# An mLSTM with a soft mixture of experts on one core: four regroupings of the instruction order

## The chip, the cores and the metric

One core of a Trainium2 chip runs the whole kernel in one launch. The metric is the device time of that core in microseconds (us), from one execution; the median of several executions is given for a kernel. Lower is better. TensorE, VectorE, ScalarE and GpSimd compute, SyncE (SP) issues the DMAs. Each engine takes its instructions in the order in which they were recorded, and waits where one needs another engine's result.

## What is computed

For 4 batches, 8 heads, 768 tokens and heads of 40 values, an mLSTM recurrence with stabilised exponential gates, its output gated and normalised; then the 320 values of a token (all heads) go through a soft mixture of 8 experts with 4 slots each.

```python
# attention part, per token t (per batch and head)
m_new  = maximum(f[t] + m, i[t])
f_stab = exp(f[t] + m - m_new);  i_stab = exp(i[t] - m_new);  m = m_new
C = f_stab * C + i_stab * outer(v[t], k[t])
n = f_stab * n + i_stab * k[t]
y[t] = sigmoid(o[t]) * (C @ q[t]) / maximum(abs(n @ q[t]), 1.0)

# soft mixture, x: 3072 tokens x 320
logits = x @ phi                                # 32 slots
d = softmax of logits over the tokens;  slot_input = d.T @ x
slot_out[e] = maximum(slot_input[e] @ w1[e], 0) @ w2[e]
c = softmax of logits over the slots;   out = c @ slot_out
```

All data is float32 (the output too). w1 and w2 are 10.5 MB each.

## The kernel before

**Steps.** The tokens of a batch are cut into 6 chunks of 128. A step is one chunk of one batch; the 24 steps go chunk by chunk with the four batches inside, so step i is chunk i // 4 of batch i % 4. Within a chunk the recurrence is done by matrices: a mask of decays times the products of queries and keys (the part inside the chunk), and the state of the earlier chunks times the queries (the part between chunks).

**What a step does, by function.** `expo(i)` (L304): TensorE multiplies two small matrices, RRt and LLt, into pe (L309), which holds the exponents of the decay mask; ScalarE makes the exponential, EWt (L311). `mix_rl(i)` (L317): ScalarE copies EWt's last column, rl, with which the keys are scaled. `scores(i)` (L347): TensorE, queries times keys into the bank psc, which has one buffer. `mix(i)` (L372): VectorE multiplies psc into EWt in place. `pv(i)` (L419): TensorE, EWt times values into the bank ph, which has one buffer. `inter(i)` (L360): TensorE, state times queries into pi; `inter_ops(i)` (L366): VectorE scales it with the decays eg into itt. `post1_ops(i)` (L427 to L431): VectorE adds itt to ph and forms the denominator's reciprocal den in three short instructions; `post2(i)` (L445): VectorE multiplies ph by the output gate sig. `gate(i)` (L456): sig times den gives the token output x; on GpSimd up to step 20 exclusive, on VectorE from there. `keys(i)` (L377): GpSimd scales the keys with rl into KRt. `state(i)` (L391, L393): TensorE, KRt times values into the bank pst; `state_dec(i)` (L399): GpSimd multiplies the state St by the decay dS; `state_ops(i)` (L406 on ScalarE for the first chunk, L407 on VectorE later): pst is added to St. `xtr(i)` (L466, L469): TensorE transposes x, ScalarE copies it to xT.

**Gates.** `gate_part` turns raw gates into the matrices' entries by scans and elementwise operations, for chunk 0, for chunks 1 and 2, and for chunks 3 to 5. The scans (L223, L228, L252) and L229 to L234 are VectorE's, L224 to L227 GpSimd's. For chunks 1 and 2, `nxt`, the first four go out before the loop and the rest, with `last_sums`, at the end of step 1. `chunk_ops(i)` puts a step's gates in place: `side` writes LLt (ScalarE, L270), `spread` writes RRt (VectorE, L277). The last chunks' operations are spread over steps 2 to 8 by the list PLATE.

**Decays.** `decays(c)`, at the end of steps 2, 4, 8, 9 and 10: TensorE transposes the gates of chunk c (L331), ScalarE makes eg of them (L332); except for the last chunk, TensorE multiplies the gates' last sums, rg (L335), and ScalarE makes dS (L336). Both products lie in one tile, pg, of the rotation pm: two PSUM buffers that pi, pt (from `xtr`), pl (the logits), pd, psl and pc share. The bank pst is 512 columns wide, of which the state's product uses 328.

**Mixture.** Groups of four steps: `logits_mm` (L474) into pl; running maximum nm (L491, L495); ScalarE's exponential dT and copy lt (L506, L514); dT transposed (L518), copied to d (L520); psl = d times x (L527), added to acc (L533). For the weights of the combination c: lt transposed, maximum subtracted (L544 to L549), exponential e (L553), the sum's reciprocal rsum (`comb_s_ops`, L574 to L576), e times rsum (`comb_n`, L583), split into a rounded part (`comb_hi`, ScalarE, L587) and a rest (`comb_lo`, GpSimd, L591), transposed into pc (L565), copied to cT (L569). In the loop a group's part of this stands in steps with i % 4 of 1, 2, 3 and 0; the multiplication by rsum stands in steps 7, 11, 15 and 19.

**The end.** Steps 22 and 23 (NL = 22, NL + 1) are written out behind the loop, with the last groups' mixture between them; then slot inputs (L882 to L907), the experts' two layers (`up`, `down`) and the combination with the output's DMAs (`combine`). The w2 weights come in 16 waves of 640 KB (`load_wave`), into buffers that the loop has done with; 11 of them are issued here. bk is the bank of psc under another name, pq and phe are that of pe.

**What sets the order.** The order is written by hand: `tc.manual_schedule()` keeps the order of recording on each engine, and the framework adds the waits for data and buffers. Waits between engines on PSUM are kept per bank: an engine that touches a bank waits until another engine's earlier access to the bank is done.

## Time and profile before

| | |
|---|---|
| median of 3 runs | 190.71 us (188.79 to 194.32) |
| the profiled execution | 188.0 us |
| its span, first to last instruction | 186.2 us |
| mean granted TensorE clock | 0.964 of full speed |
| moved by DMA | 47.42 MB, 255 GB/s over the span |

The profile is of one execution of the kernel, so the rows add up to 186.2 us, and the 1.8 us to 188.0 lie around them. Times in rows are us from the first instruction. PE is TensorE's matmul, PEld its weight load, DVE VectorE, ACT ScalarE, POOL GpSimd; a name such as EWt is a tile of the program, L372 a line of the kernel. A row's bracket tells how long the engine stood idle just before, and whose end released it. Idle time of an engine that nobody waits for costs nothing.

### The profile page before, as it was taken

Reading aid. Unit: us, or ns where it says so; the run is one execution under the profiler, and the core shown is the slowest. Engines: PE = TensorE matmul, PEld = TensorE weight load, DVE = VectorE, ACT = ScalarE, POOL = GpSimd, SP = SyncE. Lnnn points to the kernel's source line nnn. Section 1 sums busy time; section 2 is a strip of 40 time slices with the busy share of each in tenths; the row PEclk is TensorE's granted clock in tenths of the full one; section 3 lists DMA queues with packets and bytes.
Section 4 is the critical chain, followed back from the end, with each engine's and each line's share of the span. In section 5 each row is a group of like instructions: output and inputs, shape, how many; then the busy total and the mean of one; then the engine's idle time right before and its main releaser. Section 6 shows DMA issues by size and latency. Waiting matters only on the chain.

```text
span 186.2 us, 6239 instructions
## 1 busy us (share of the span) xinstructions
PE 159.5 (86%) x2594; PEld 117.3 (63%) x2594; DVE 124.1 (67%) x305; ACT 85.8 (46%) x205; POOL 63.1 (34%) x90
## 2 busy tenths in 40 slices
PE   7986657996896989997999989999978798999950
PEld 2554546885586867766877778777764442478740
DVE  6863786279879957479775997779688366323450
ACT  4888643656374544544445336634303432004340
POOL 8038058646336544046434443434211201100000
PEclk9999978999999699999999999999997899999996
DMA  5999998679968899766899989783869998001996
GB/s 173 306 315 367 314 328 279 193 218 376 268 199 271 217 338 302 227 220 175 303 344 293 278 253 364 210 274 100 256 214 364 362 364 267 0 4 57 293 305 194
DMA packets 27323, 47.42 MB, mean 255 GB/s; under 512 B 3184, under 2 KB 18288, under 8 KB 27296
## 3 DMA queue, kind: packets, MB, share of 16 engines
q1 hardware_dynamic: 27296, 47.03, 80.1%
q8 instruction: 20, 0.33, 0.8%
q14 instruction: 7, 0.06, 0.1%
HBM read 42.80 MB, written 4.23 MB: 253 GB/s over the span
## 4 chain that ended last, share of the span: by engine, by line
PE 69%; DVE 13%; ACT 8%; issue 4%; POOL 2%; DVEq 0%; ACTq 0%; POOLq 0%
PE psc L347 11%; PE ph L419 10%; PE pe L309 7%; PE pi L360 6%; PE pt L466 5%; PE pso L945 5%; PE pw L173 4%; DVE EWt L372 3%; PE pst L391 3%; PE po L975 3%; PE bk L917 2%; PE phh L917 2%; DVE RRt L277 2%; PE psl L527 2%; ACT xT L469 2%
## 5 line engine op out<-in xcount | busy, mean ns | idle before, releaser
L456 POOL TENSOR_TENSOR Xt<-sig,den 128x320 f32<-128x320 f32 x20 | 17.1, 856 | 53.1 <-DVE sig L445 53.1
L372 DVE TENSOR_TENSOR EWt<-psc,EWt 128x1024 f32<-128x1024 f32 x24 | 29.2, 1216 | 5.3 <-ACT rl L317 4.6
L347 PE MATMUL psc<-KQt 64*128 64x128 f32 (+1 forms) x384 | 28.6, 290 | 4.0 <-DVE EWt L372 1.9
L469 ACT COPY xT<-pt 128x384 f32<-128x384 f32 x23 | 10.9, 479 | 38.8 <-PE pt L466 38.8
L419 PEld LDWEIGHTS ph<-KVt,EWt 128*64 128x64 f32 x704 | 23.4, 143 | 8.2 <-issue 5.8
L347 PEld LDWEIGHTS psc<-KQt 64*128 64x128 f32 (+1 forms) x384 | 24.1, 192 | 6.4 <-DVE EWt L372 2.8
L311 ACT ACTIVATE EWt<-pe 128x512 f32<-128x512 f32 x48 | 26.0, 593 | 4.6 <-PE pe L309 4.4
L419 PE MATMUL ph<-KVt,EWt 128*64 128x41 f32 x704 | 26.0, 236 | 1.2 <-issue 1.2
L360 PE MATMUL pi<-St,KQt 104*64 104x82 f32 x320 | 15.7, 241 | 0.0
L377 POOL TENSOR_TENSOR KRt<-KVt,rl 128x320 f32<-128x320 f32 x20 | 14.7, 736 | 2.2 <-DMA KVt<-in_kv_dram 1.3
L366 DVE TENSOR_TENSOR itt<-pi,eg 128x328 f32<-128x328 f32 x20 | 10.0, 499 | 6.9 <-PE pi L360 5.7
L360 PEld LDWEIGHTS pi<-St,KQt 104*64 104x64 f32 x320 | 12.5, 136 | 2.3
L391 PE MATMUL pst<-KVt,KRt 128*64 128x41 f32 x160 | 12.8, 230 | 0.8 <-POOL KRt L377 0.7
L466 PE MATMUL pt<-cst,Xt 128*128 128x128 f32 x63 | 11.5, 296 | 2.0 <-DVE itt L366 2.0
L399 POOL TENSOR_TENSOR St<-St,dS 104x328 f32<-104x328 f32 x16 | 12.7, 794 | 0.1
L391 PEld LDWEIGHTS pst<-KVt,KRt 128*64 128x64 f32 x160 | 11.5, 142 | 1.3 <-POOL KRt L377 0.8
L309 PE MATMUL pe<-RRt,LLt 128*64 128x512 f32 (+1 forms) x24 | 9.0, 459 | 3.7 <-DVE RRt L277 2.3
L427 DVE TENSOR_TENSOR ph<-ph,itt 128x328 f32<-128x328 f32 x18 | 9.1, 504 | 3.6 <-PE ph L419 3.6
L591 POOL TENSOR_TENSOR E<-e,E 128x256 fp32r<-128x256 f32 x7 | 5.1, 735 | 14.4 <-ACT E L587 7.8
L393 PE MATMUL pst<-KVt,KRt 128*40 128x41 f32 x160 | 9.9, 207 | 0.0
L445 DVE SCALAR_TENSOR_TENSOR sig<-sig,ph 128x320 f32<-128x320 f32 x22 | 9.6, 438 | 0.0
L466 PEld LDWEIGHTS pt<-cst,Xt 128*128 128x128 f32 x63 | 6.7, 144 | 3.5 <-DVE itt L366 1.2
(227 smaller groups left out, 273.7 us busy)
## 6 DMA issues: line engine op xcount, KB each, us to landing
w<-in_w_dram SPq DMA_DIRECT2D x20, 512.0 KB, 6.2
KVt<-in_kv_dram SPq DMA_DIRECT2D x24, 324.0 KB, 4.7
KQt<-in_qk_dram SPq DMA_DIRECT2D x24, 320.0 KB, 5.5
w<-in_w_dram SPq DMA_DIRECT2D x7, 640.0 KB, 6.9
sig<-in_og_dram SPq DMA_DIRECT2D x6, 640.0 KB
out_dram<-ob SPq DMA_DIRECT2D x5, 384.0 KB, 4.1
KQt<-in_w_dram SPq DMA_DIRECT2D x2, 640.0 KB, 5.3
EWt<-in_w_dram SPq DMA_DIRECT2D x2, 640.0 KB, 9.6
```

The lines of the kernel that those rows point to most:

```text
L309: nc.tensor.matmul(pe[0:x, n], l[0:k, n * LH:n * LH + x], r[0:k, :, n * LH:n * LH + LH], start=True, stop=True)
L311: nc.scalar.activation(w[:, 0:2, :, n * LH:n * LH + LH].rearrange("p e j t -> p j e t"), pe[:, n].rearrange("p (j e) t -> p j e t", e=2), ...
L347: nc.tensor.matmul(psc[:, e, j], t[r0:r1, 1, j], t[r0:r1, 0, j], start=True, stop=True)
L360: nc.tensor.matmul(pi[z, j], q[0:104, 0, j, z], St[0:104, i % B, j], start=True, stop=True, tile_position=(0, 64 * u))
L372: nc.vector.tensor_tensor(w, pscs.pop(i), w, ALU.mult)
L377: e.tensor_tensor(kr[i][:, 24:].rearrange("p (j e d) -> p j e d", e=2, d=D), KV[i % NK][:, 0:DM].rearrange("p (j e d) -> p j e d", e=2, d= ...
L391: nc.tensor.matmul(pst[0:64, j, 0:V1], kr[i][:, h * D:h * D + 64], v_of(i, h), start=True, stop=True)
L399: nc.gpsimd.tensor_tensor(s, s, dS[0:104, i // B, i % B].unsqueeze(2).broadcast_to([104, HP, 2 * V1]), ALU.mult)
L419: nc.tensor.matmul(ph_[z, h * V1:(h + 1) * V1], w[:, h % 2, h // 2, z], v_of(i, h), start=True, stop=True, tile_position=(0, TW * u))
L456: e.tensor_tensor(x_of(i)[:, h0 * D:h1 * D].rearrange("p (h d) -> p h d", d=D), s1_of(i)[:, h0:h1], dens[i][:, h0:h1].unsqueeze(2).broadca ...
L466: nc.tensor.transpose(pt[:, kc, :], x[:, o:o + P], ident)
L469: nc.scalar.copy(xT[i // GRP][:, :, i % GRP, :], pt)
```

## The change

Four parts:

1. In step 1 the rest of the gates of chunks 1 and 2 (`nxt`, `last_sums`) is recorded before `mix(2)` instead of at the step's end, and `chunk_ops(4)` before `post1_ops(1)`.
2. `decays` puts its two products into the free columns of pst instead of a tile of pm, and issues both before ScalarE reads the first.
3. In the loop `comb_n`, e times rsum, runs on GpSimd.
4. Behind the loop: `gate` of steps 20, 21 and 22 on GpSimd; `mix(23)` and `pv(22)` ahead of the inter products' use; `pv(23)` and the transposition pc of group 3 ahead of the transpositions of x; the logits of group 4 in pst, their maximum, exponential, transposition, psl and acc behind the last gates; `inter(23)` behind `pv(22)`.

```diff
@@ decays
-        t = pp.tile([P, L + 16], F32, tag="pm", name=f"pg{c}", bufs=2)
+        t = pst_t[:, HP * 2 * V1:HP * 2 * V1 + L + 16]
         nc.tensor.transpose(t[:, 0:L], y, ident)
+        if c + 1 < NCH:
+            nc.tensor.matmul(t[:, L:L + 16], ccol(C_LE, 128), rg.pop(c), start=True, stop=True)
         nc.scalar.activation(eg[:, c].rearrange("p (q a) h -> p q a h", q=2),
...
         if c + 1 < NCH:
-            nc.tensor.matmul(t[:, L:L + 16], ccol(C_LE, 128), rg.pop(c), start=True, stop=True)
             nc.scalar.activation(dS[:, c].rearrange("p b j -> p (b j)"), t[:, L:L + 16], AF.Exp)
@@ the loop
         cmb = i > 2 * GRP - 1 and i % GRP == 0
+        if i == 1:
+            emit(nxt)
+            last_sums(1, CD - 1)
         mix(i + 1)
...
+        if i == 1:
+            chunk_ops(4)
         emit(post1_ops(i) + ([lambda: post2(i)] if i > EARLY else []))
         emit(inter_ops(i + 1))
-        if i == 1:
-            emit(nxt)
-            last_sums(1, CD - 1)
-            chunk_ops(4)
         chunk_ops(i + 4)
...
             emit(comb_s_ops(gi, run["e"]))
-            comb_n(run["e"])
+            comb_n(run["e"], nc.gpsimd)
@@ behind the loop
     mix(NL)
-    gate(i - 1)
+    gate(i - 1, nc.gpsimd)
     comb_lo(run["e"])
...
     pv(i)
     scores(NL + 1)
     inter(NL)
-    emit(inter_ops(NL))
-    inter(NL + 1)
-    pl4 = moe_pl(gl - 1, "pm")
     post1(i)
     post2(i)
+    gate(i, nc.gpsimd)
+    mix(NL + 1)
+    emit(inter_ops(NL))
     pv(NL, pp.tile([P, 2, 512], F32, tag="pe", name="phe")[:, 0])
-    mix(NL + 1)
+    inter(NL + 1)
     emit(inter_ops(NL + 1))
-    emit(moe_nm_ops(gl - 1, pl4))
-    ex_dT(gl - 1)
-    al4 = run["al"]
-    ex_lt(gl - 1, pl4)
-    xtr(i - 1)
-    moe_dT(gl - 1)
     while len(w2_sb) < 9:
         load_wave()
-    gate(i)
 
     bk = pp.tile([P, 2, 512], F32, tag="psc", name="bk")
     pv(NL + 1, bk[:, 1])
+    comb_h(gl - 2, comb_T("ph"))
+    while len(w2_sb) < 15:
+        load_wave()
+    pl4 = pst_t[:, HP * 2 * V1:HP * 2 * V1 + P]
+    logits_mm(gl - 1, pl4, range(GRP))
+    xtr(i - 1)
     xtr(i)
-    psl4 = pp.tile([P, DM + 1], F32, tag="ph", name="psl4")
-    moe_psl(gl - 1, psl4)
-    while len(w2_sb) < 16:
-        load_wave()
...
     late(NL)
-    gate(NL)
+    gate(NL, nc.gpsimd)
     xtr(NL)
     j = NL + 1
     late(j)
-    moe_acc(gl - 1, psl4, al4)
...
         nc.scalar.copy(xT[gl][:, k0:k0 + n, GRP - 1, :], pt)
+    emit(moe_nm_ops(gl - 1, pl4))
+    ex_dT(gl - 1)
+    al4 = run["al"]
+    ex_lt(gl - 1, pl4)
     pl = bk[:, 1, 0:P]
     logits_mm(gl, pl, [0, 1, 2])
     logits_mm(gl, pl, [3])
...
-    pc3 = comb_T(pc=pq[:, 0].rearrange("p (j t) -> p j t", j=GRP))
+    moe_dT(gl - 1)
+    psl4 = moe_psl(gl - 1, pp.tile([P, DM + 1], F32, tag="ph", name="psl4"))
+    load_wave()
+    lt4 = run["lt"]
     emit(moe_nm_ops(gl, pl))
...
-    nc.tensor.transpose(pd2[0], run["lt"], ident)
+    nc.tensor.transpose(pd2[0], lt4, ident)
+    moe_acc(gl - 1, psl4, al4)
...
     up(0, range(1))
-    comb_h(gl - 2, pc3)
```

How the rows of three places moved (the lines of the changed kernel are one to three higher, and the numbers in names are the program's own).

VectorE in step 1, before: the third mix (psc_259), the three instructions of post1(1), the gates of chunks 1 and 2 (g, gf, hi_t, Y, rg), RRt of chunk 1, the fourth mix.

```order
L372 TENSOR_TENSOR EWt<-psc_259,EWt 128x1024
L429 TENSOR_REDUCE ph_282<-ph_282 128x8
L430 TENSOR_SCALAR ph_282<-ph_282 128x8
L431 RECIPROCAL den_316<-ph_282 128x8
L228 SCALAR_TENSOR_TENSOR g<-rst,gf_93 128x256
L229 SCALAR_TENSOR_TENSOR gf_93<-gf_93,cst,g 128x256
L233 CAST hi_t<-gf_93 128x256
L234 SCALAR_TENSOR_TENSOR Y<-hi_t,cst,gf_93 128x256
L321 TENSOR_TENSOR rg_324<-cst,g 128x32
L277 TENSOR_TENSOR RRt<-Y,cst 32x1024
L372 TENSOR_TENSOR EWt<-psc_299,EWt 128x1024
```

The same stretch of VectorE after the change:

```order
L228 SCALAR_TENSOR_TENSOR g<-rst,gf_93 128x256
L229 SCALAR_TENSOR_TENSOR gf_93<-gf_93,cst,g 128x256
L233 CAST hi_t<-gf_93 128x256
L234 SCALAR_TENSOR_TENSOR Y<-hi_t,cst,gf_93 128x256
L321 TENSOR_TENSOR rg_284<-cst,g 128x32
L373 TENSOR_TENSOR EWt<-psc_259,EWt 128x1024
L277 TENSOR_TENSOR RRt<-Y,cst 32x1024
L430 TENSOR_REDUCE ph_288<-ph_288 128x8
L431 TENSOR_SCALAR ph_288<-ph_288 128x8
L432 RECIPROCAL den_325<-ph_288 128x8
L373 TENSOR_TENSOR EWt<-psc_305,EWt 128x1024
```

The five gate rows stand ahead of the third mix, and RRt ahead of post1(1).

GpSimd in steps 7 and 8, before: the keys of step 8 (rl_674), the gate of step 7, the state's decay and the keys of step 9, then the rest of group 0's combine weights.

```order
L377 TENSOR_TENSOR KRt<-KVt,rl_674 128x320
L456 TENSOR_TENSOR Xt<-sig_269,den_818 128x320
L399 TENSOR_TENSOR St<-St,dS 104x328
L377 TENSOR_TENSOR KRt<-KVt,rl_763 128x320
L591 TENSOR_TENSOR E<-e_751,E 128x16x16
```

The same stretch of GpSimd after the change:

```order
L378 TENSOR_TENSOR KRt<-KVt,rl_672 128x320
L584 TENSOR_TENSOR e_749<-e_749,rsum_825 128x128
L457 TENSOR_TENSOR Xt<-sig_269,den_816 128x320
L400 TENSOR_TENSOR St<-St,dS 104x328
L378 TENSOR_TENSOR KRt<-KVt,rl_761 128x320
L592 TENSOR_TENSOR E<-e_749,E 128x16x16
```

The multiplication by rsum is new there, ahead of the gate, the decay and the keys. On VectorE it is gone.

TensorE behind the loop, before: scores(23), inter(22) and inter(23) (pi), the logits of group 4 (pl), pv(22) (phe), x of step 20 transposed, dT of group 4 transposed (pd), pv(23) (bk), x of step 21 transposed (xy), psl of group 4, x of step 22 transposed.

```order
L347 MATMUL psc_1968<-KQt 128x128 x8
L360 MATMUL pi_1977<-St,KQt 64x82 x8
L360 MATMUL pi_1987<-St,KQt 64x82 x8
L474 MATMUL pl_1996<-xT_1715,cst 32x128 x12
L419 MATMUL phe<-KVt,EWt 64x41 x16
L466 MATMUL pt_2044<-cst,Xt 128x128 x3
L518 MATMUL pd_2050<-cst,dT_2038 128x128
L419 MATMUL bk<-KVt,EWt 64x41 x16
L466 MATMUL pt_2079<-cst,xy 128x128 x3
L527 MATMUL psl_2084<-Xt,d_2052 32x321 x4
L466 MATMUL pt_2106<-cst,w_3_1729 128x128 x3
```

The same stretch of TensorE after the change, down to the logits of group 5 (bk) and prow:

```order
L348 MATMUL psc_1963<-KQt 128x128 x8
L361 MATMUL pi_1972<-St,KQt 64x82 x8
L420 MATMUL phe<-KVt,EWt 64x41 x16
L361 MATMUL pi_2007<-St,KQt 64x82 x8
L420 MATMUL bk<-KVt,EWt 64x41 x16
L566 MATMUL pc<-identr,E 128x128 x4
L475 MATMUL pst<-xT_1710,cst 32x128 x12
...
L475 MATMUL bk<-xT_2072,cst 32x128 x12
L519 MATMUL pd_2130<-cst,dT_2109 128x128
L528 MATMUL psl_2134<-Xt,d_2132 32x321 x4
L860 MATMUL prow<-cst,nm_2141 1x128
```

Both value products (phe, bk) stand ahead of all transpositions, and pd and psl of group 4 have moved behind the logits of group 5.

## Rows read from the trace of the kernel before

**Rows 1.** The profile's page, the chain of work that ended last: shares of the span by engine.

```profile
PE 69%; DVE 13%; ACT 8%; issue 4%; POOL 2%; DVEq 0%; ACTq 0%; POOLq 0%
```

**Rows 2.** The busy time by stage: start and end of the stage in us, its length, then for TensorE (PE), its weight loads (PEld), VectorE (DVE), ScalarE (ACT) and GpSimd (POOL) the busy us and the number of instructions, then the granted TensorE clock (1.00 is full), the DMA share and GB/s.

```profile
0.00:66.00 66.00, 53.79 (x797) 40.09 (x799) 47.84 (x102) 40.19 (x92) 32.79 (x44) 0.95 0.87 271
...
84.00:134.90 50.90, 48.49 (x910) 38.23 (x908) 40.32 (x98) 23.37 (x53) 20.51 (x31) 1.00 0.84 259
```

**Rows 3.** The timeline of steps 0 to 2, 14 to 28 us. Columns, here and in the timelines below: start in us, duration in us (of the whole row, where it has several instructions), engine, line, operation, output<-inputs, shape, count, and in brackets the idle time of the engine just before and what ended it.

```profile
15.14 1.14 POOL L227 TENSOR_SCALAR gf<-gf,cst 128x256 f32<-128x256 f32 x1
...
17.75 1.23 DVE L372 TENSOR_TENSOR EWt<-psc,EWt 128x1024 f32<-128x1024 f32 x1 [2.98 <-ACT rl L317]
...
20.58 0.64 DVE L228 TENSOR_TENSOR_SCAN g<-rst,gf 128x256 f32<-128x256 f32 x1
...
21.25 0.19 ACT L317 COPY rl<-EWt 128x8 f32<-128x8 f32 x1
...
22.62 1.21 DVE L277 TENSOR_TENSOR RRt<-Y,cst 32x1024 fp32r<-32x1024 f32 x1
...
23.98 0.65 PE L309 MATMUL pe<-RRt,LLt 128*64 128x512 f32 x2 [2.31 <-DVE RRt L277]
...
24.89 0.86 DVE L445 SCALAR_TENSOR_TENSOR sig<-sig,ph 128x320 f32<-128x320 f32 x2
...
25.86 1.94 PE L419 MATMUL ph<-KVt,EWt 128*64 128x41 f32 x32 [1.23 <-issue]
```

**Rows 4.** The timeline of GpSimd and of the scan on VectorE behind it, 30 to 40 us (steps 3 and 4).

```profile
30.67 0.73 POOL L377 TENSOR_TENSOR KRt<-KVt,rl 128x320 f32<-128x320 f32 x1
...
35.65 0.72 POOL L456 TENSOR_TENSOR Xt<-sig,den 128x320 f32<-128x320 f32 x1 [1.53 <-DVE sig L445]
...
37.97 1.56 POOL L227 TENSOR_SCALAR gf<-gf,cst 128x384 f32<-128x384 f32 x1
...
39.57 0.96 DVE L228 TENSOR_TENSOR_SCAN g<-rst,gf 128x384 f32<-128x384 f32 x1 [1.11 <-POOL gf L227]
```

**Rows 5.** The view of one tile: time from issue to landing of the one load into KVt that was issued at 21.75 (step 4's keys and values).

```profile
DMA to landing us min/median/max: 6.6/6.6/6.6
```

**Rows 6.** The timeline around the decays, steps 2, 5, 8, 9 and 10.

```profile
32.50 0.39 PE L335 MATMUL pg<-rg,cst 128*128 128x16 f32 x2 [0.92 <-ACT eg L332]
...
49.84 0.52 PE L466 MATMUL pt<-cst,Xt 128*128 128x128 f32 x3 [0.88 <-DVE itt L366]
...
67.74 0.39 PE L335 MATMUL pg<-rg,cst 128*128 128x16 f32 x2 [0.56 <-ACT eg L332]
...
68.17 0.18 ACT L336 ACTIVATE dS<-pg 128x16 f32<-128x16 f32 x1 [0.48 <-PE pg L335]
...
69.84 0.29 DVE L491 TENSOR_REDUCE nmx<-pl 128x1 f32<-128x128 f32 x1 [1.60 <-PE pl L474]
...
74.52 0.40 PE L335 MATMUL pg<-rg,cst 128*128 128x16 f32 x2 [0.49 <-ACT eg L332]
...
80.61 0.33 PE L331 MATMUL pg<-cst,g 128*128 128x128 f32 x1 [0.46 <-ACT xT L469]
```

**Rows 7.** The busy time by stage, columns as in rows 2, of 2 us while TensorE does pv(2) and scores(4).

```profile
26.00:28.00 2.00, 2.00 (x34) 1.92 (x35) 1.20 (x2) 0.37 (x2) 2.00 (x3) 0.50 1.03 246
```

**Rows 8.** The timeline of steps 11 and 12 (84 to 89 us), then one row each of steps 15/16 and 19.

```profile
84.99 0.73 POOL L399 TENSOR_TENSOR St<-St,dS 104x328 f32<-104x328 f32 x1
...
85.25 1.19 DVE L575 TENSOR_SCALAR rsum<-rsum 128x4 f32<-128x4 f32 x1
...
86.89 1.22 DVE L372 TENSOR_TENSOR EWt<-psc,EWt 128x1024 f32<-128x1024 f32 x1
...
88.21 1.16 PE L347 MATMUL psc<-KQt 64*128 64x128 f32 x16 [1.10 <-issue]
...
109.34 1.16 PE L347 MATMUL psc<-KQt 64*128 64x128 f32 x16 [0.83 <-PE ph L419]
...
127.78 0.17 DVE L575 TENSOR_SCALAR rsum<-rsum 128x4 f32<-128x4 f32 x1
```

**Rows 9.** The timeline of steps 21 to 23 and of what follows, 132 to 147 us.

```profile
132.68 1.13 PE L419 MATMUL ph<-KVt,EWt 128*64 128x41 f32 x32
...
134.83 1.36 PE L360 MATMUL pi<-St,KQt 104*64 104x82 f32 x32
...
135.67 0.50 DVE L366 TENSOR_TENSOR itt<-pi,eg 128x328 f32<-128x328 f32 x1 [1.98 <-PE pi L360]
...
139.12 0.28 DVE L491 TENSOR_REDUCE nmx<-pl 128x1 f32<-128x128 f32 x1
...
139.92 0.50 DVE L427 TENSOR_TENSOR phe<-phe,itt 128x328 f32<-128x328 f32 x1
...
141.63 0.49 DVE L456 TENSOR_TENSOR w<-sig,den 128x320 f32<-128x320 f32 x1
...
142.48 1.30 PE L527 MATMUL psl<-Xt,d 128*32 128x321 f32 x8
...
143.95 0.55 DVE L533 SCALAR_TENSOR_TENSOR acc<-acc,al,psl 128x321 f32<-128x321 f32 x1 [0.22 <-PE psl L527]
...
144.41 0.56 DVE L456 TENSOR_TENSOR w<-sig,den 128x160 f32<-128x160 f32 x2
...
146.09 1.10 PE L474 MATMUL bk<-xT,cst 128*32 128x128 f32 x24 [0.46 <-ACT xT L842]
```

## The prediction

> **What bounds the kernel now.** I read the chain of work that ended last, then the busy time by stage, then the timeline wherever TensorE waits. TensorE carries 69% of the chain and VectorE 13% [rows 1]. From 84 to 134.9 TensorE is busy 48.49 of 50.90 us at the full clock, 2.4 GHz; from 0 to 66 only 53.79 of 66.00, at a granted clock of 0.95 [rows 2]. So time can be won in the first 66 us, at single waits of the loop, and behind 134.9. The edits touch all three.
>
> I write mix(i), pv(i) and so on for step i's call. Durations come from the profiled execution: span 186.2, time 188.0.
>
> **Gates of chunks 1 and 2 ahead of the third mix.** GpSimd finishes their gates at 15.14 + 1.14 = 16.28; VectorE first sits behind mix(2), which waits 2.98 for ScalarE, and takes the gates up at 20.58; they end at 22.62, 2.04 later [rows 3]. TensorE waits 2.31 for RRt, and pv(2) waits again, until post2 (sig, 24.89) has read the bank that it overwrites; it starts at 25.86 [rows 3].
> Now: gates 16.28 to 18.32, mix(2) to 19.55, RRt (1.21) to 20.75. mix(2) is 0.6 later, but the product that overwrites its scores, scores(3), stands behind pv(1) on TensorE and came later than 19.55: no cost. The three short instructions of post1(1) end before 21.44, when ScalarE's rl (21.25 + 0.19) releases mix(3); mix(3) ends at 22.65, the two sig (0.86) at 23.5. pv(2) starts 2.3 us earlier.
> This doesn't all stay. Behind it stands GpSimd: keys(4) at 30.67, three gate operations, gate(3) at 35.65 after an idle 1.53, and the multiply at 37.97, whose end releases VectorE's scan at 39.57 [rows 4]. keys(4) needs the load issued at 21.75, landed 6.6 later, at about 28.4 to 28.7 [rows 5], and the DMA queue is no earlier there, since that load's buffer comes free at the same time as before. From 28.7 the same GpSimd work without the idle 1.53 takes 37.97 + 1.56 - 30.67 - 1.53 = 7.33: to 36.0 instead of 39.53. I take **3.3**, 0.2 less than the difference, for port waits. Bounds: 0 if transfers hold all, 4.0 if GpSimd didn't hold it (2.3, the 0.92 that TensorE waited for ScalarE in decays(1) [rows 6], and 0.8 for pv(2), whose 1.94 would be about 1.1 at the full clock, as later steps have it).
> Clock: after 2.31 and 1.23 idle it was 0.50, which is 1.2 GHz, at 26 to 28 [rows 7]; the wait of 1.10 at 88.21 [rows 8] lies in a stretch at 1.00 [rows 2]. With about 0.45 and 0.8 left I expect the full clock; if it drops, GpSimd's path above is the same.
>
> **Decays in the state's bank.** Five times TensorE transposes the gates, and four of them it multiplies too, with ScalarE's reading between: it waited 0.92, 0.56 and 0.49 for that reading, and 0.46 for a buffer [rows 6]. Now both products follow each other and take no buffer from the rotation of two. At step 2 this is in the 3.3. At step 4 VectorE's chain from the scan at 39.57 decides, so 0. At step 5 the transposes' wait of 0.88 for itt becomes one for ScalarE's copy of d: 0 to 0.88, I take **0.5**. At steps 8 to 10 TensorE is the bound: 0.56 + 0.49 + 0.46, nearly whole, **1.45** (bounds 0.9 and 1.6).
> The added wait: the state's addition on VectorE (L407) now waits until ScalarE has read the decays. dS ends at 68.17 + 0.18 = 68.35 today, having waited 0.48 for the second product; behind the addition on VectorE stands nmx, idle for 1.60 until 69.84 [rows 6]: hidden, and some 0.5 a step if that cover were gone.
> The Trainium skill (PSUM — Partial Sum Buffer, "PSUM bank collisions raise a hardware error") says that two engines must not touch one bank and quadrant at once, other columns or not. That is the rule that speaks against sharing the bank. By it alone the additions of three steps would come 0.5 late each, 1.5 in all; by the row they end in idle time, and the sum stays.
>
> **Combine weights on GpSimd.** Four times VectorE's multiply L583 (0.29 by its neighbours of the same shape) goes. More goes with it: at 85.25 the tiny L575 takes 1.19 while GpSimd runs 84.99 and its next operation; with GpSimd idle it takes 0.17 at 127.78 [rows 8]. The new order puts the multiply ahead of GpSimd's gate, decay and keys, so GpSimd is idle, waiting for this very reciprocal, when L575 runs. mix at 86.89 then starts about 1.24 earlier, and TensorE's wait of 1.10 at 88.21 goes; at step 15 its 0.83 at 109.34 [rows 8] goes likewise. At steps 7 and 19 the trace shows no wait of TensorE ahead of psc: 0. Term **1.9**, bounds 0 and 2.3. The new multiply has no row on GpSimd: 0.29 (VectorE, same shape) to 0.74 (twice the size on GpSimd); I take 0.4. Queued behind its wait are gate, decay and keys (some 2.2 us); those keys are read two steps later, so nobody waits. The cast of E on ScalarE now waits for GpSimd; it comes no later than today, since the reciprocal is earlier.
> The Trainium skill (Perfetto Trace Analysis, "Optimizing Scalar/DVE Operations") warns that GpSimd and VectorE share a read port, so moving work between them might not help. The trace agrees that the port costs time (1.19 against 0.17); by the rule the term is 0, which is a rival below.
>
> **The tail.** Today VectorE's itt waits 1.98 at 135.67 for both inter products, and everything behind it follows [rows 9]. pv(21) ends at 132.68 + 1.13 = 133.81. From 135.67 to 139.12 VectorE needs 3.45 for two itt, the normalisation and mix(23). Now the same starts at 133.85; inter(23) comes after inter(22) (0.68, half of 1.36), and pv(22) (1.13): 134.83 + 0.68 + 1.13 + 0.68 = 137.35, so itt(23) ends near 137.9. From 139.92 to the end of the last gate at 144.41 + 0.56 = 144.97 are 5.05; the gate of 141.63 moves to GpSimd (0.41 by start to start), the acc at 143.95 moves behind (about 0.7 with its wait). Last gate: 137.9 + 3.95 = 141.85, **3.1** earlier. GpSimd's gate (0.72, as 35.65 in [rows 4]) is done before VectorE ends. The logits (24 matmuls from 146.09, 1.10, partly below full clock) run 0.3 faster if the clock holds. Against it: the transposition of dT, its copy and psl now stand between these logits and prow: psl is 0.75 at full clock (estimate; the row at 142.48 has 1.30 at the lower one), and acc stands ahead of nM. Cost 0.7 beyond what waits anyhow. Term 3.1 + 0.3 - 0.7 = **2.7**; bounds 2.0 (psl at 1.30) and 3.4.
> The weights of the last part: SP's load into KQ's second piece waits for inter(23), some 1.2 later, and the EW loads for pv(23), some 3 earlier. First use is 25 us on; 0.
>
> **Sum.** 3.3 + 0.5 + 1.45 + 1.9 + 2.7 = 9.85; 188.0 - 9.85 = 178.15. The profiled execution lies 2.7 under the median of the runs shown, 190.71; I add half of that, 1.35, here and to each rival: **179.5**.
>
> **Rivals.**
> - Front held: transfers and GpSimd eat the gates' gain, 3.3 and 0.5 go: 181.95, reported 183.3. For: the DMA share is 0.87 over the first 66 us [rows 2], and keys(4) starts as its load lands. Against: a share of 0.87 leaves over 8 us free.
> - Transfers bind the whole loop: all 7.15 before the tail is lost: 185.3, reported 186.6. For: the share of 0.84 up to 134.9 [rows 2]. Against: TensorE, not a load, ends nearly every wait there.
> - The port moves its price: GpSimd's operations, later now, stretch mix or the state's addition, and the 1.9 goes: 180.05, reported 181.4. Against: mix reads PSUM, and its 1.22 in [rows 8] is the same with GpSimd busy.
> - Slower: TensorE, waiting oftener for VectorE where it used to wait for ScalarE, drops to 1.2 GHz in the stretch 84 to 134.9. pv takes 1.94 at that level and 1.13 at the full one [rows 3, 9]: 0.7 more per us. 14 us of its work at the low level cancel all; half of the 48.49 costs 17: about 195. It decides from an idle stretch such as 2.31 plus 1.23; I expect none over 1.2.
>
> **How the numbers follow.** Forecast 0.55, front held 0.20, transfers 0.12, port 0.09, slower clock 0.04. Low end: all upper bounds, 4.0 + 0.9 + 1.6 + 2.3 + 3.4 = 12.2, are 175.8, without the 1.35; rounded to 175. High end 187, just past the transfers' case. About 2% is what a measurement of this kernel tells from no change, so the border is 186.9: faster 0.55 + 0.20 + 0.09 = 0.84, same 0.12, slower 0.04.
>
> **What would show it.** Right: pv(2) near 23.5 at full clock; VectorE's scan g near 36 with GpSimd as releaser; no wait of TensorE at L335; L575 at 0.17 in all loop steps and no wait ahead of psc at steps 11 and 15; logits of the last group some 3.4 nearer to inter(22) than now; prow behind psl. Wrong: keys waiting for KVt loads by several us; a granted clock of 0.5 in the loop; psl and prow at the low clock; a span above 183.

## The result: 180.83 us where 179.5 was forecast

Four executions of the changed kernel took 178.44 to 181.99 us, median 180.83; the kernel before, beside them, 190.1. The ratio is 0.945, interval 0.930 to 0.961. It uses the executions within 1.5% of a kernel's fastest; medians here are over all. Timed again beside other kernels, the changed kernel had a median of 183.03 in six executions, ratio 0.949 (0.938 to 0.960); over all ten 181.8. Its profiled execution took 178.44, with a span of 176.7: 9.5 less than before, where the terms made 9.85.

That agreement hides misses that cancel. Executions start differently: the constants landed 1.0 us later here (ScalarE's first cast of them begins at 5.18, before at 4.16), so I count from the start of pv(0), 12.83 before and 13.85 after, in the rows of L419 (L420).

| start, us behind pv(0) | before | after | after less before | gained since the line above | forecast |
|---|---|---|---|---|---|
| pv(2) | 13.03 | 11.37 | -1.66 | 1.66 | 2.3 |
| pv(5) | 32.48 | 28.18 | -4.30 | 2.64 | 3.3 with the line above |
| pv(7) | 42.97 | 39.16 | -3.81 | -0.49 | 0.5 |
| pv(12) | 73.15 | 66.80 | -6.35 | 2.54 | 1.45 |
| pv(21) | 119.85 | 112.52 | -7.33 | 0.98 | 1.9 |
| end of the span | 173.37 | 162.85 | -10.52 | 3.19 | 2.7 |

The page of the changed kernel, shares of the chain of waits by engine, where [rows 1] had no DMA worth a per cent:

```profile
PE 65%; DVE 13%; DMA 9%; POOL 3%; ACT 3%; issue 3%; POOLq 0%; DVEq 0%; SPq 0%
```

Busy time by stage, columns as in [rows 2]:

```profile
0.00:66.00 66.00, 55.39 (x887) 41.41 (x889) 50.07 (x107) 42.86 (x102) 35.11 (x48) 1.00 0.94 286
...
84.00:134.90 50.90, 48.75 (x927) 38.70 (x926) 39.46 (x101) 22.91 (x52) 20.56 (x34) 1.00 0.86 263
```

The clock stays at 1.00 over the first 66 us (0.95 before), and the DMA share has risen from 0.87 to 0.94: 286 GB/s instead of 271. The chain's 9% on DMA is new: loads have taken the place of some of the waits removed.

The front, against [rows 3]; timeline of steps 0 to 2:

```profile
14.85 0.73 POOL L378 TENSOR_TENSOR KRt<-KVt,rl 128x320 f32<-128x320 f32 x1
...
16.16 1.14 POOL L227 TENSOR_SCALAR gf<-gf,cst 128x256 f32<-128x256 f32 x1
...
17.28 0.73 POOL L378 TENSOR_TENSOR KRt<-KVt,rl 128x320 f32<-128x320 f32 x1
...
17.34 1.22 DVE L228 TENSOR_TENSOR_SCAN g<-rst,gf 128x256 f32<-128x256 f32 x1 [1.54 <-POOL gf L227]
...
18.86 0.81 POOL L378 TENSOR_TENSOR KRt<-KVt,rl 128x320 f32<-128x320 f32 x1 [0.85 <-POOL KRt L378]
...
19.11 0.71 DVE L233 CAST hi_t<-gf 128x256 fp32r<-128x256 f32 x1
...
20.26 0.19 DVE L321 TENSOR_TENSOR rg<-cst,g 128x32 f32<-128x32 f32 x1
...
20.36 1.22 DVE L373 TENSOR_TENSOR EWt<-psc,EWt 128x1024 f32<-128x1024 f32 x1
...
23.32 0.68 PE L309 MATMUL pe<-RRt,LLt 128*64 128x512 f32 x2
...
25.22 1.13 PE L420 MATMUL ph<-KVt,EWt 128*64 128x41 f32 x32 [1.23 <-issue]
```

pe(4) waits no more and pv(2) is at full clock, 1.13 where 1.94 stood. But the gates take 17.34 to 20.45, 3.11 where they took 2.04: the scan has 1.22, before 0.64, beside GpSimd's keys at 17.28, and the cast hi_t has 0.71, before 0.29, beside those at 18.86. Before, GpSimd was idle from 18.58 (6.92 ahead of its next operation at 25.50), so while VectorE did the gates. So pv(2) gained 1.66, not 2.3.

Steps 4 and 5, against [rows 4]:

```profile
33.35 0.73 POOL L400 TENSOR_TENSOR St<-St,dS 104x328 f32<-104x328 f32 x1
...
35.42 0.74 POOL L378 TENSOR_TENSOR KRt<-KVt,rl 128x320 f32<-128x320 f32 x1 [1.34 <-DMA KVt<-in_kv_dram]
...
36.14 1.57 POOL L227 TENSOR_SCALAR gf<-gf,cst 128x384 f32<-128x384 f32 x1
...
37.74 0.96 DVE L228 TENSOR_TENSOR_SCAN g<-rst,gf 128x384 f32<-128x384 f32 x1 [3.12 <-POOL gf L227]
...
40.69 0.49 DVE L367 TENSOR_TENSOR itt<-pi,eg 128x328 f32<-128x328 f32 x1
...
41.24 0.86 PE L475 MATMUL pl<-xT,cst 128*32 128x128 f32 x24 [1.43 <-DVE itt L367]
...
42.03 1.13 PE L420 MATMUL ph<-KVt,EWt 128*64 128x41 f32 x32
```

The scan g was forecast at 36.0, which is 23.2 behind pv(0); it is at 23.9, since GpSimd waits 1.34 for the load of step 5's keys. Yet pv(5) is 4.30 earlier, which the scan doesn't explain (2.85 earlier against pv(0)). The rest is at step 4, in rows of the kernel before that I had passed over:

```profile
42.53 0.49 DVE L366 TENSOR_TENSOR itt<-pi,eg 128x328 f32<-128x328 f32 x1
...
43.08 0.33 PE L331 MATMUL pg<-cst,g 128*128 128x128 f32 x1 [1.25 <-DVE itt L366]
...
45.31 1.13 PE L419 MATMUL ph<-KVt,EWt 128*64 128x41 f32 x32
```

There the transposition of the gates waited for the buffer that VectorE's itt frees, and ScalarE's reading, the second product and pe stood behind it: 2.29 from itt's end (42.53 + 0.49) to pv(5). Now only the logits wait for itt (41.24), and from its end (40.69 + 0.49) to pv(5) it is 0.85.

The decays of step 8, against the 0.56 of [rows 6], and the waits ahead of scores(12), (16) and (17), on TensorE:

```profile
62.44 0.27 PE L331 MATMUL pst<-cst,g 128*128 128x128 f32 x1
...
62.54 0.29 PE L333 MATMUL pst<-rg,cst 128*128 128x16 f32 x2
...
62.69 0.51 PE L566 MATMUL pc<-identr,E 128*128 128x128 f32 x4
...
72.52 1.16 PE L348 MATMUL psc<-KQt 64*128 64x128 f32 x16 [1.32 <-DMA KQt<-in_qk_dram]
...
93.55 1.16 PE L348 MATMUL psc<-KQt 64*128 64x128 f32 x16 [0.81 <-DVE ph L430]
...
98.74 1.16 PE L348 MATMUL psc<-KQt 64*128 64x128 f32 x16 [0.56 <-DVE EWt L373]
```

The transposition and pc of step 8 in the kernel before:

```profile
66.91 0.27 PE L331 MATMUL pg<-cst,g 128*128 128x128 f32 x1
...
67.98 0.51 PE L565 MATMUL pc<-identr,E 128*128 128x128 f32 x4
```

From the transposition to pc are 0.25 us, before 67.98 - 66.91 = 1.07: 0.82 saved, more than the wait of 0.56, because the second product no longer starts by itself: it now begins 0.10 behind the transposition, which takes 0.27. No wait stands ahead of scores(14) and (18), where 1.10 and 0.83 stood [rows 8], and the addition to rsum has 0.17 each time; GpSimd's new multiplication takes 0.40, as I took it. But TensorE waits 1.32 for the load of step 12's queries and keys, and 0.81 and 0.56 later. The row at 93.55 names VectorE, which had released the bank at 90.81; the same wait in four kernels below (u_comb, u_tail, u_decays, after_again) is released by the load into KQt. The 0.56 is a true wait for VectorE's mix(16). What SP issued ahead of the load that scores(12) waits for:

```profile
61.35 0.38 SPq L159 DMA_DIRECT2D sig<-in_og_dram  x1
...
61.78 0.42 SPq L164 DMA_DIRECT2D w<-in_w_dram  x1
...
62.25 0.43 SPq L692 DMA_DIRECT2D w<-in_w_dram  x1
...
62.78 0.93 SPq L153 DMA_DIRECT2D KVt<-in_kv_dram  x1
...
63.75 0.45 SPq L149 DMA_DIRECT2D KQt<-in_qk_dram  x1
```

In step 8 the output gates (sig, 640 KB), a w1 load (512 KB), a wave (640 KB) and the values stand ahead of it. Its use came 8.8 us behind its issue.

The tail, against [rows 9]:

```profile
134.72 0.56 DVE L457 TENSOR_TENSOR w<-sig,den 128x160 f32<-128x160 f32 x2
...
136.24 1.10 PE L475 MATMUL bk<-xT,cst 128*32 128x128 f32 x24 [0.46 <-ACT xT L838]
...
137.96 0.75 PE L528 MATMUL psl<-Xt,d 128*32 128x321 f32 x8 [0.35 <-ACT d L521]
...
138.63 0.27 PE L860 MATMUL prow<-cst,nm 128*1 128x128 f32 x1
```

And prow in the kernel before:

```profile
147.93 0.27 PE L857 MATMUL prow<-cst,nm 128*1 128x128 f32 x1 [0.28 <-DVE nm L495]
```

From pv(21) the last gate ends 8.91 behind (126.37 to 135.28), before 12.29: 3.4 earlier, forecast 3.1; the logits 3.5 earlier; prow 3.0 (12.26 for 15.25), so the wedge of psl cost 0.5, forecast 0.7. Part of this is the clock, which falls at 141.5 in the profile of the kernel before. The three profiles below that have the old tail and no fall up to prow (u_tail, before_fill, waves_before) have the last gate 11.96 and prow 14.75 or 14.76 behind pv(21). Against them the last gate comes 3.05 earlier and prow 2.5.

### The profile page after: what moved, and what is told of

Same layout as the page of the kernel before. It is cut to its first block, busy times and chain, and to the rows that moved or that the text cites. A ratio compares the mean times of both kernels' runs of the same rounds, so it can differ in the third digit from the quotient of the medians.

```text
span 176.7 us, 6243 instructions
## 1 busy us (share of the span) xinstructions
PE 153.7 (87%) x2594; PEld 114.1 (65%) x2594; DVE 119.7 (68%) x298; ACT 84.9 (48%) x205; POOL 66.4 (38%) x97
## 4 chain that ended last, share of the span: by engine, by line
PE 65%; DVE 13%; DMA 9%; POOL 3%; ACT 3%; issue 3%; POOLq 0%; DVEq 0%; SPq 0%
PE psc L348 11%; PE ph L420 7%; PE pi L361 7%; PE pso L949 5%; DMA KQt<-in_qk_dram 5%; PE pe L309 5%; PE pw L173 4%; DMA KVt<-in_kv_dram 4%; DVE EWt L373 4%; PE pt L467 4%; PE pst L392 3%; PE po L979 3%; PE bk L921 3%; PE phh L921 3%; DVE RRt L277 2%
## 5 line engine op out<-in xcount | busy, mean ns | idle before, releaser
L348 PE MATMUL psc<-KQt 64*128 64x128 f32 (+1 forms) x384 | 27.9, 285 | 6.0 <-DVE EWt L373 3.4
L348 PEld LDWEIGHTS psc<-KQt 64*128 64x128 f32 (+1 forms) x384 | 23.4, 188 | 8.6 <-DVE EWt L373 4.6
L457 POOL TENSOR_TENSOR Xt<-sig,den 128x320 f32<-128x320 f32 x21 | 17.7, 847 | 28.6 <-DVE sig L446 28.6
L420 PEld LDWEIGHTS ph<-KVt,EWt 128*64 128x64 f32 x704 | 22.3, 138 | 7.9 <-issue 4.6
L420 PE MATMUL ph<-KVt,EWt 128*64 128x41 f32 x704 | 24.9, 232 | 1.2 <-issue 1.2
L392 PE MATMUL pst<-KVt,KRt 128*64 128x41 f32 x160 | 12.3, 226 | 1.4 <-ACT St L407 0.8
L173 PE MATMUL pw<-wz 128*128 128x512 bf16 x24 | 8.3, 521 | 1.2 <-DVE wz L168 1.2
```

The costliest lines, as they stand in the source:

```text
L173: nc.tensor.matmul(pw, wz[:, 0:P], wz, start=True, stop=True)
L348: nc.tensor.matmul(psc[:, e, j], t[r0:r1, 1, j], t[r0:r1, 0, j], start=True, stop=True)
L392: nc.tensor.matmul(pst[0:64, j, 0:V1], kr[i][:, h * D:h * D + 64], v_of(i, h), start=True, stop=True)
L420: nc.tensor.matmul(ph_[z, h * V1:(h + 1) * V1], w[:, h % 2, h // 2, z], v_of(i, h), start=True, stop=True, tile_position=(0, TW * u))
L457: e.tensor_tensor(x_of(i)[:, h0 * D:h1 * D].rearrange("p (h d) -> p h d", d=D), s1_of(i)[:, h0:h1], dens[i][:, h0:h1].unsqueeze(2).broadca ...
```

## The experiments

Times are medians of six executions (before_fill twelve), the ratio is to the kernel before, timed beside them on the same chip (medians of it 191.17 beside the first four rows, 191.79 beside the next four, 191.94 beside the last four, where no ratio is given). In the expectations the scores behind scores(12) are counted one too low: those called scores(13), (15), (16) and (17) are scores(14), (16), (17) and (18).

| kernel | median | lowest to highest | ratio |
|---|---|---|---|
| u_front | 183.36 | 182.15 to 187.69 | 0.973 |
| u_decays | 183.80 | 181.39 to 185.51 | 0.972 |
| u_comb | 179.57 | 177.50 to 181.52 | 0.952 |
| u_tail | 183.85 | 181.34 to 188.56 | 0.967 |
| after_again | 183.03 | 177.82 to 186.21 | 0.949 |
| waves_off_sig | 176.51 | 175.54 to 177.84 | 0.937 |
| waves_u_comb | 179.08 | 177.52 to 180.16 | 0.949 |
| before_fill | 191.93 | 186.31 to 196.72 | 0.996 |
| waves_before | 190.38 | 188.45 to 192.90 | |
| waves_undec | 182.61 | 179.25 to 186.64 | |
| waves_unfront | 178.23 | 177.35 to 180.47 | |
| waves_w1_psl | 176.28 | 174.74 to 179.20 | |

**u_front: the gates late again.**

```diff
-        if i == 1:
-            emit(nxt)
-            last_sums(1, CD - 1)
         mix(i + 1)
...
-        if i == 1:
-            chunk_ops(4)
         emit(post1_ops(i) + ([lambda: post2(i)] if i > EARLY else []))
         emit(inter_ops(i + 1))
+        if i == 1:
+            emit(nxt)
+            last_sums(1, CD - 1)
+            chunk_ops(4)
```

> The changed kernel with its first part undone: the gates of chunks 1 and 2 stand at the end of step 1 again, the other three parts stay. In the changed kernel pv(5) starts 28.18 us behind pv(0), in the kernel before 32.48. My theory, this part makes nearly all of the front's gain: pv(5) about 32 behind pv(0), the scan g released by GpSimd some 3.5 later than in the changed kernel against the same pv(0), TensorE at 1.2 GHz again while it does pv(2); the time 2.5 to 4 above the changed kernel, less than the 4.3 of the front if waits for loads further on (1.32 at scores(12), 0.81 at scores(15) in the changed kernel) shrink by it. Rival, loads bind the loop: those waits vanish and the whole costs under 1.5. Rival, the decays' new bank made the front's gain: pv(5) stays under 29.5.

```profile
39.72 0.96 DVE L228 TENSOR_TENSOR_SCAN g<-rst,gf 128x384 f32<-128x384 f32 x1 [1.68 <-POOL gf L227]
```

pv(5) stood 31.17 behind pv(0), the scan g 26.87 and released by GpSimd, both 3.0 later than in the changed kernel; the wait of 2.31 was back, and the clock was 0.54 from 25.0 to 32.5. So the part is worth 3.0 at pv(5), and by the path over GpSimd and the scan: under the 4.3 that I then gave it, near the 3.3 of the prediction, the rest being the decays'. The third answer, that the bank made the front's gain, holds for that rest alone. The waits for loads did not vanish (2.15 at scores(12)), against the second. The median is 0.3 and 2.5 above the two of the changed kernel, too uneven to decide between the first two; the ratio is 0.973 where that has 0.945 and 0.949.

**u_decays: the old tile.**

```diff
-        t = pst_t[:, HP * 2 * V1:HP * 2 * V1 + L + 16]
+        t = pp.tile([P, L + 16], F32, tag="pm", name=f"pg{c}", bufs=2)
...
-        if c + 1 < NCH:
-            nc.tensor.matmul(t[:, L:L + 16], ccol(C_LE, 128), rg.pop(c), start=True, stop=True)
         nc.scalar.activation(eg[:, c].rearrange("p (q a) h -> p q a h", q=2),
...
         if c + 1 < NCH:
+            nc.tensor.matmul(t[:, L:L + 16], ccol(C_LE, 128), rg.pop(c), start=True, stop=True)
```

> The changed kernel with its second part undone: the decays' products lie in a tile of the rotation of two again, ScalarE reads between them. My theory: TensorE waits for ScalarE at steps 2, 8 and 9 (0.92, 0.56 and 0.49 in the kernel before) and for a buffer at step 10 (0.46); from pv(7) to pv(11) about 1.5 more of TensorE's waits, and the time 1 to 1.5 above the changed kernel. Rival, loads bind there: the wait of scores(12) for its load (1.32 in the changed kernel) shrinks by as much, pv(12) comes at most 0.4 later against pv(0), and the time is the same.

All the waits were back (0.92, 0.56, 0.49, 0.46), and 1.38 at step 4. In this execution the clock also fell to 0.57 from 31.0 to 35.0 and to 0.51 from 41.5 to 52.0, and pv(5) came at 31.92. scores(12) waited no more. The median is 0.8 and 3.0 above the two of the changed kernel, yet with two falls in its profile this run sizes nothing; waves_undec does.

**u_comb: the multiplication by rsum on VectorE again.**

```diff
-            comb_n(run["e"], nc.gpsimd)
+            comb_n(run["e"])
```

> The changed kernel with its third part undone: the multiplication by rsum is VectorE's again in the loop. My theory as predicted: L576 (add to rsum) takes 0.7 to 1.2 at steps 11 and 15 beside GpSimd's work, TensorE waits about 1.0 ahead of scores(13) and 0.8 ahead of scores(17), and the time is 1.9 above the changed kernel. What the trace of the changed kernel suggests instead: it has new waits of 0.81 ahead of scores(15) and 0.56 ahead of scores(16), which go if the earlier steps are slower, so the time is only about 0.8 above. Rival, the port moves its price: no difference at all, since GpSimd's multiplication stretches other VectorE work by as much.

The waits ahead of scores(14) and (18) were back, 0.83 each, and the addition to rsum took up to 0.69. A third one came, 1.13 ahead of scores(10), behind the addition of step 7, where the prediction had 0. Even so the median is no higher than the changed kernel's, and the ratios, 0.952 and 0.945 to 0.949, can't be told apart. The waits for the loads did not all shrink: scores(12) waited 0.23, scores(16) 1.74 for KQt, and the clock was 0.57 from 95 to 99. In the changed kernel this part gains nothing that I can measure.

**u_tail: the old order behind the loop** (the diff's last part taken back whole).

> The changed kernel with its fourth part undone: everything behind the loop in the order of the kernel before. From the start of pv(21) to the end are 50.33 us in the changed kernel and 53.52 in the kernel before. My theory: 53.5 again, the time 2.7 to 3.2 above the changed kernel, and nothing in the loop moves. Rival, the loop's earlier end makes part of the tail's gain (weights land earlier against the work): 51.5 to 52.5, the time 1.2 to 2.2 above.

The end lies 54.83 behind the start of pv(21), 4.5 more than the 50.33 of the changed kernel. prow comes 14.76 behind it (15.25 before, 12.26 after): 2.5 of the 4.5. The rest stands behind prow, from where it takes 40.07 to the end here, 39.02 in before_fill and 38.07 in the changed kernel; the clock was 0.52 from 142.0 to 145.5, where the first layer runs. Of the four profiles with the old tail three have a fall between the loop and the last 10 us (this one, before from 141.5, waves_before from 149.0) and before_fill has none; of the ten with the new tail none has one. The median is 0.8 and 3.0 above the two of the changed kernel, the lowest time 2.9 and 3.5 above theirs; that is nearer to the first answer.

**after_again, waves_off_sig, waves_u_comb, before_fill**, on one chip. The second moves the weight waves out of the steps that load sig, the third has that and VectorE's multiplication, the fourth is the kernel before with idle work in two waits:

```diff
-WVN = {4: 1, 8: 1, 12: 1, 18: 1}
+WVN = {6: 1, 10: 1, 14: 1, 18: 1}
```

```diff
+            run["ph"] = ph_
...
+        if i == 2:
+            for _ in range(16):
+                nc.tensor.transpose(pst_t[:, 336:464], ident, ident)
         expo(i + 2)
...
         pv(i)
+        if i == 7:
+            ph7 = run["ph"]
+            for _ in range(11):
+                nc.tensor.transpose(ph7[:, 336:464], ident, ident)
         scores(i + 2)
```

> The changed kernel unaltered, timed again beside the other three on one chip. If TensorE's falls to 1.2 GHz are a matter of the single execution, its profile may show one where the first profile of it shows none; I expect at most one, costing about 2, and a ratio to the kernel before of 0.94 to 0.955. Rival: the gain seen first was luck, ratio 0.965 or more.

The profile fell on the slowest of the six executions, 186.21. It shows one thing that makes this kernel's times spread: scores(16) waited for its load, and then came the longest stretch at 1.2 GHz that any profile has in the loop. pv(14) to pv(16) took 18.36, in the first profile 10.53: one fall with its wait cost 7.8, where I had expected about 2.

```profile
95.92 2.08 PE L348 MATMUL psc<-KQt 64*128 64x128 f32 x16 [3.27 <-DMA KQt<-in_qk_dram]
```

```profile
95.50:109.50 14.00, 13.58 (x138) 11.00 (x138) 6.00 (x15) 2.38 (x7) 2.75 (x5) 0.51 0.45 138
```

> The changed kernel with the three weight waves that stand in steps 4, 8 and 12, where the load of the gates sig (640 KB) stands too, moved to steps 6, 10 and 14. My theory, loads take back part of what the change won: TensorE's waits of 1.32 ahead of scores(12) and 0.81 ahead of scores(15), and GpSimd's of 1.34 for the keys of step 5, shrink to under 0.3 each, and the time is 1 to 2.5 under the changed kernel. Rival, the loads are only late by their volume, wherever the wave stands: the waits turn up two steps later (scores(14) to scores(17)), time the same.

The waits ahead of scores(12) and (16) are gone; pv(21) comes 98.94 behind pv(2), in the changed kernel 101.15. The times lie within 2.3 us, the median is 4.3 and 6.5 under the two of the changed kernel, the lowest time 2.3 under its lowest, the ratio 0.937 (0.932 to 0.942) against 0.945 and 0.949. (Here I count from pv(2): the clock of this execution was 0.57 from 10.5 to 14.5, and pv(0) started 1 to 2 late.) The loads were late by their place in the queue. GpSimd's wait for step 5's keys stayed, 1.17: the wave of step 4 is not what delays it.

> The kernel with the moved waves, and the multiplication by rsum on VectorE again. My theory: where loads don't bind, the third part is worth what its waits say (about 1.1 at step 9, 0.9 at step 13, 0.9 at step 17 in pv's distances), so this is 1.9 to 2.9 above the kernel with the moved waves. Rival: 0 to 0.8 above it, the waits of the loads come back in the place of those on VectorE.

2.6 above the kernel with the moved waves, as the first answer has it; pv(21) 102.40 behind pv(2), 3.5 more, of which scattered waits for loads (0.94 at scores(6), 1.23 at scores(14)) are a part. So the third part has its value where the loads leave room, and lost it in the changed kernel.

> The kernel before with idle work for TensorE in two of its waits: 16 transpositions of the identity ahead of pe(4) in step 2 (the wait of 2.31 for RRt) and 11 ahead of scores(9) in step 7 (the wait of 1.47), written to columns that nobody reads. The waits themselves stay. My theory, the waits let the clock fall to 1.2 GHz, which costs the kernel before 1.5 to 2 each time: no fall at 25 to 29 and at 60 to 63, pv(3) about 18.5 behind pv(0) in place of 20.51, and the time 2 to 3.5 under the kernel before. Rival, the fall doesn't hang on these waits: the clock falls as before, time the same or up to 0.5 more.

```profile
39.40 0.96 DVE L228 TENSOR_TENSOR_SCAN g<-rst,gf 128x384 f32<-128x384 f32 x1 [1.12 <-POOL gf L227]
```

```profile
25.00:29.00 4.00, 2.41 (x46) 1.99 (x48) 3.86 (x8) 1.79 (x5) 2.12 (x3) 1.00 1.02 325
...
43.50:47.50 4.00, 3.97 (x58) 2.86 (x58) 2.66 (x4) 2.32 (x7) 2.12 (x2) 0.57 1.05 357
...
60.00:64.00 4.00, 3.18 (x71) 2.65 (x69) 3.71 (x10) 2.10 (x6) 2.62 (x4) 1.00 0.78 240
```

The falls at 25 and 60 are gone while the instructions waited for are as late as before (RRt holds TensorE 0.41 more after the idle work), and pv(3) stands 18.97 behind pv(0), before 20.51. The fall at 25 is in all four kernels whose wait there is unfilled, so it hung on TensorE standing still. For the one at 60 this isn't shown: waves_before has the wait unfilled, 1.46, and no fall either. The scan g stands 25.19 behind pv(0) here, with the gates late as ever, and 26.74 in the kernel before: the fall at 25 costs 1.55 there. But another fall came at 43.5, behind the waits of 1.25 and 0.29 at step 4, and the median is that of the kernel before. Fewer falls in one place were not a shorter time. Whether the new fall came by chance or because of the filling stays open.

**waves_before, waves_undec, waves_unfront:** the moved waves put into the kernel before, and into the changed kernel with its second or first part undone (the edits are those above).

> The kernel before with the three weight waves moved from steps 4, 8 and 12 to steps 6, 10 and 14, nothing else. My theory: the loads bind only since the change has shortened the steps, so the kernel before gains nothing from the move: ratio 0.99 to 1.01. Rival, the waves in the steps of sig cost the kernel before as much: ratio 0.975 to 0.985, and the move is worth the same in both.

190.38 beside 191.94 by medians, 188.45 beside 187.65 by the lowest: no gain that can be told from none, as I thought. So the loads became a bound with the change, as far as these times can tell.

```profile
63.95 1.16 PE L347 MATMUL psc<-KQt 64*128 64x128 f32 x16 [1.13 <-issue]
```

This profile has the wait of 1.46 ahead of scores(9) and no fall at 60, and then this wait ahead of scores(10), which the profile of the kernel before didn't have. pv(8) comes 5.78 behind pv(7), before 7.03, but pv(7) to pv(12) take 29.76 (29.77 in before_fill), before 30.18: of the 1.25 that the fall cost, 0.8 lay where TensorE waits for VectorE otherwise.

> The kernel with the moved waves, with the second part (the decays' bank) undone. As predicted the part is worth 0.5 at step 5 and 1.45 at steps 8 to 10. From the traces I now add 1.44 at step 4, where the transposition of the gates waits for the buffer that itt frees and pe(6) stands behind it, and 0.9 at step 2: 3.5 to 4.5 above the kernel with the moved waves, more where the clock falls. Rival: the value predicted, 1.5 to 2.2 above.

182.61, 6.1 above waves_off_sig. By position pv(21) comes 102.65 behind pv(2), 3.7 more, with no fall of the clock in the loop of this profile. pv(5) is 1.3 later, step 5 gives 0.5 back, and the gaps from pv(8) to pv(11) are 0.85, 0.83 and 0.68 longer: 3.3 up to pv(11), against the 1.95 of the prediction. The last 0.4 are not the decays': scores(18) waits 1.05 there. The 0.92 is back at step 2, but the scan g stands 12.16 behind pv(2), with the part 12.34, so that wait is swallowed before it. The profile is of the fastest execution, 179.25 at a mean clock of 0.989; the other five have 0.975 to 0.938, and what lowered it there no row shows.

> The kernel with the moved waves, with the first part (the gates of chunks 1 and 2 early) undone. The predicted value of the part was 3.3. pv(5) should stand about 31 behind pv(0) against 26.8 to 28 with it, and the clock fall at 25 (after the wait of 2.31 for RRt), as in both kernels that have this order and no filling: 3 to 4 above the kernel with the moved waves. Rival, given back in the loop through earlier loads: 1 to 2 above.

pv(5) stands 30.99 behind pv(0) and the clock fell from 24.5 to 32.0, as expected. By position the part is worth 3.0 (pv(2) 1.66 later as in the first table, and from there to pv(5) 17.96 for 16.63). By the medians it is 1.7, which is the rival's 1 to 2. But the loop gave nothing back in the profiles: pv(5) to pv(21) take 82.20, with the part 82.31. The profile of waves_off_sig lost its lead by its late start; whether its other executions did too no row shows.

**waves_w1_psl: a try for a faster kernel**, with the moved waves and these two edits.

```diff
-W1N = (3,) + 17 * (1,)
+W1N = (3, 1, 0, 0) + 16 * (1,)
...
-    psl4 = moe_psl(gl - 1, pp.tile([P, DM + 1], F32, tag="ph", name="psl4"))
-    load_wave()
...
     nc.tensor.transpose(prow, nmf, ident)
+    psl4 = moe_psl(gl - 1, pp.tile([P, DM + 1], F32, tag="ph", name="psl4"))
+    load_wave()
```

> A try for a faster kernel: the changed kernel with the moved waves; the w1 loads of steps 2 and 3 moved to the loop's end; prow ahead of psl of group 4. Expected: GpSimd's wait for the keys of step 5 (1.17 with the moved waves) goes, scan g and pv(5) come about 1.2 earlier; prow and pcol come 0.3 earlier against the logits of group 5; in all 1 to 1.5 under the kernel with the moved waves. Rival, the scan is held by GpSimd's own work and the weights come late at the end: no gain, or a wait of TensorE for weights in the experts' first layer.

```profile
33.92 0.74 POOL L378 TENSOR_TENSOR KRt<-KVt,rl 128x320 f32<-128x320 f32 x1
...
36.25 0.96 DVE L228 TENSOR_TENSOR_SCAN g<-rst,gf 128x384 f32<-128x384 f32 x1 [1.74 <-POOL gf L227]
...
136.15 0.27 PE L858 MATMUL prow<-cst,nm 128*1 128x128 f32 x1 [0.48 <-DVE nm L496]
```

GpSimd no longer waits for the keys, and the scan g stands 22.5 behind pv(0), before the forecast 23.2: with the load out of the way GpSimd's own work holds it, as the prediction had it. But the gaps ahead of pv(17), pv(21) and pv(22) are 0.70, 0.82 and 0.31 longer than in the kernel with the moved waves: TensorE waits 0.63, 0.76 and 0.23 there, the last by the row for KQt, the others with VectorE named as at 93.55 above. I take these for the w1 loads come back; no run shows it apart. prow stands 1.85 behind the logits, in the changed kernel 2.39: 0.5 gained, but not kept, since the experts' first layer (L921) starts 12.53 behind pv(22), and 12.42 without the edits. The median is 176.28 and 176.51 without these two edits: the same. These two kernels are the fastest of the study.

## Why the prediction was right, point by point

- **The gates ahead of the third mix** (3.3): right in size, 3.0 by u_front and waves_unfront, and in its path over GpSimd and the scan. The first half of the path was too short: gates beside GpSimd's keys take 3.11, not 2.04. The second half was long by the load, which is the "front held" rival at about 0.7 of its 3.8 (23.9 for 23.2). And "if it drops, GpSimd's path above is the same" was wrong: 1.55 of the scan's 2.85 is the clock's fall that is gone (before_fill, gates late and no fall).
- **The decays' bank** (0.5 + 1.45): the step that failed. "At step 4 VectorE's chain from the scan at 39.57 decides, so 0" looked at who came last and not at what stood behind it on TensorE: 1.44 there. At step 5 the 0.5 never came: the copy of d costs TensorE 0.45 where itt cost 0.88, scores(7) now waits 0.68 for mix(6), and pv(5) to pv(7) got 0.49 longer. At steps 8 to 10 each wait counted alone, without the product that starts afresh behind it: 2.4 for 1.45. All in all 3.3 for 1.95 (waves_undec). The added wait of the state's addition on VectorE shows once, 0.31 at step 9, in idle time, so the 1.5 that I had priced for the shared bank did not come. The rule behind that price, that two engines must not touch one bank and quadrant at once, is the Trainium skill's (PSUM — Partial Sum Buffer, "PSUM bank collisions raise a hardware error").
- **The combine weights** (1.9): mechanism right, to the 0.17 and the 0.40, but one place was missing. "At steps 7 and 19 the trace shows no wait of TensorE ahead of psc: 0" read a stretch at the low clock: waves_before and before_fill, whose clock holds there, wait 1.13 ahead of scores(10), and so does u_comb. Beside u_comb the changed kernel is 1.08, 0.90 and 0.90 faster in the steps 8, 12 and 16. Loads took it back, a small part of what the rival of the transfers (0.12) had: the part is worth 2.6 by the medians with the waves moved, and nothing measurable in the changed kernel. The rival of the port is out here. The same price came at the gates instead: 1.22 for 0.64 beside GpSimd's 0.73. The Trainium skill (Perfetto Trace Analysis, "Optimizing Scalar/DVE Operations") warns that GpSimd and VectorE share a read port.
- **The tail** (2.7): 3.2 in the profile: the last gate 3.4, the logits 0.1 more, psl's wedge -0.5, and 0.2 behind prow. At the full clock in both, the last gate is 3.05 (forecast 3.1) and prow 2.5; the rest was the fall at 141.5 in the kernel before. The logits themselves take 1.10 in both, so the 0.3 that I gave them for the clock did not come there.
- **The loads**: "TensorE, not a load, ends nearly every wait there" was true of a kernel with longer steps. About 2.2 up to pv(21) went to them, by waves_off_sig.
- **The clock**: I bounded it at 0.8 for pv(2). The kernel before falls twice in the loop of its profile: the first fall costs 1.55 at the scan g, the second 0.4 from pv(7) to pv(12) (waves_before, before_fill). I had not looked for either in this size: [rows 2] gave the mean of 0.95 and I opened only one of its two stretches.
- **The allowance of 1.35** for the median: it goes with the clock as well. Over 40 executions of the kernel before, 187.51 at a mean granted clock of 0.976 to 200.13 at 0.882, time and clock have a correlation of -0.96; which of the two moves the other it doesn't say.

So terms too small (decays, combine weights, tail) and what loads took back cancelled, and that the number came out within 1.3 us is in part luck. Its inner sum was right for the front and the tail alone, and in both a share was the clock's.

## What to carry to other kernels

A wait removed in a kernel with a DMA share of 0.87 is worth its length only while the loads keep up: look in the new order at which load stands behind the bulk ones in its queue, since moving three weight waves by two steps was worth as much here as a whole part of the change (2.2 by position, 4.3 to 6.5 by the medians). Where a wait goes, count what stood behind it on the waiting engine too, the instructions in between and a pipeline that starts afresh: 0.82 for a wait of 0.56. A step read at the low clock can hide a wait: ahead of scores(10) it read 0, and 1.13 wherever the clock held. And test a sum by positions, part against part, before calling it confirmed: ours was right within 1.3 us with two of its terms off by 1.35 (decays) and 1.9 (combine weights, in the changed kernel).
